# Earlier zeros for the PE fillers, two more fillers, and masks built by selections alone

## The chip, the cores and the metric

One core of a Trainium2 chip runs the whole program in one launch. The metric is the device time of that launch in microseconds (us). A kernel is run several times, and its time is the median of its runs. One further execution is recorded by the hardware profiler; every duration and start below is from that execution.

## The reference, cut to what matters

Four layers work on x (2048 tokens of 448 numbers, bfloat16). Layers 0 and 2 are attention over a local, dilated window, layers 1 and 3 are a bilinear GLU. Each adds its result to x.

```python
def A(x, wqkv, wo):                       # 16 heads of 28
    q, k, v = split(x @ wqkv)
    idx = pos[:, None] - 2 * arange(8)    # 8 keys: this token and every second one before it
    logits = einsum(q, k[idx]) * 28 ** -0.5, -1e9 where idx < 0
    return (softmax(logits) @ v[idx]) @ wo
def B(x, w_gate, w_up, w_down):           # F = 1792
    return ((x @ w_gate) * (x @ w_up)) @ w_down
x = x + A(layernorm(x)); x = x + B(layernorm(x))
x = x + A(layernorm(x)); x = x + B(layernorm(x))
```

## The kernel before

The kernel holds x in SBUF as 16 blocks of 128 tokens, even tokens in the first eight and odd tokens in the last eight, so that a dilation of two becomes a plain local window of eight. Each layer is cut into chunks of 256 or 512 tokens. `SEQ` gives the order in which chunks are planned, but what each engine runs, and in which order, is written out: `ORDER` has a list of operation numbers for each of the five queues (TensorE "pe", ScalarE "act", VectorE "dve", GpSimd "pool", SyncE "sp"), and `BANKS` gives the PSUM banks of each matmul group. An operation's number is its position in the sequence of `sc.add` calls. There is no planner left: an engine takes its list from front to back, and before each operation waits on semaphores for what that operation depends on. A dependence on an earlier operation of the same engine is also waited for by semaphore, except on TensorE. The `est` and `prio` arguments are read by nobody when an order is written out.

What comes before the first attention chunk matters here:

- SyncE issues the loads: x in five pieces, the rows of `wqkv` for V (`WV`), and those for Q and K into `stage`, which is the tile `hT` before the GLU uses it (line 444, four loads `("stg", c)`).
- VectorE takes five memsets, then the layer norm of the first blocks: `bn_stats` (line 582), `bn_aggr` (584), and the scaling into `xn_sb` (603). ScalarE makes `rstd` between them (585, 587).
- TensorE transposes the scaled blocks through an identity matrix (`ident`, lines 613 and 617). ScalarE or VectorE copies the result to `xnTa` (624, 627).
- VectorE and ScalarE spread the staged weights into the padded layout `WQK` (521), six copies and two. The first matmuls of Q and K wait for all eight and for the transposed blocks.
- TensorE has nothing to do at first. It runs `WARM + FILL` filler matmuls of 128 by 512 on `warm`, a slice of `hT` that VectorE sets to zero (line 513, operations 47 to 62): eleven ahead of the first transposes, three ahead of the second, two ahead of the third. Their results are never read.
- GpSimd sets constants and builds three masks `MK` (128 keys by 72 queries, kind 0 for the first group, 2 for the one over the middle, 1 for all others). The exponentials of the attention are cut by a minimum with the mask (line 853): very large where a key is in the window, zero elsewhere. The five parts of the masks are made in `MT`, also a slice of `hT`: one memset, then 16 selections of 128 by 72 (`affine_select`, line 491) in five chains, then three additions (495) that put the half for the first 64 keys and the half for the last 64 together. GpSimd's list runs the chains interleaved, with the other constants between them; the identity's memset and selection stand in the middle. The first writes of `hT` by the GLU wait for the masks (`war`), because `MT` lies there.

On TensorE almost every later operation is a pair of matmuls on the two row halves of the array, issued by the helper `pair` (line 351), so that line 351 covers Q and K, V, gate and up, down, and the output projection.

Of the kernel before, what the change touches and what calls it, by code (L numbers as in the profile page):

```python
# [57 lines left out]
WARM = 8  # L58
FILL = 8
# [36 lines left out]
def grp_nc(g):  # L96
# [8 lines left out]
        "47 48 49 50 51 52 53 54 55 56 57 112 58 59 60 109 61 62 127 210 130 211 240 133 136 241 204 228 205 229 200 234 201 154 235 230 198 231 202 199 151 "  # L105
        "203 232 157 160 233 215 193 354 178 355 249 352 220 353 350 175 184 351 181 254 244 496 245 498 196 497 499 575 500 576 501 571 266 572 267 271 356 "
        "369 357 370 502 276 503 379 373 569 374 570 573 574 401 384 308 302 305 314 288 311 289 320 326 338 317 323 396 526 335 397 406 520 329 521 332 515 "
        "341 516 344 345 548*3.5/346 347 531 588 418 589 419 448 445 457 451 463 543 460 544 553*1.2.4.5/442 472 469 475 454 599*1.3.5/466 481 593 565 478 566 "
        "484 485 594 486 487 665 604*1.2.4.5/662 677 689 674 490 621*2.4.5/491 668 492 742 736 493 737 743 738 626*3.5/740 616 739 617 686 741 701 671 680 759 "
        "692 760 698 683 695 638 755 639 704 756 705 765 706 707 779*1.3.5/826 710 838 823 711 829 712 713 770 784*1.2.4.5/835 841 853 850 847 859 896 900 820 "  # L110
        "901 897 980 898 894 899 895 977 989 796 918 986 797 1001 1013 919 992 998 1004 913 1010 914 832 924*5/844 856 1016 983 862 929 946 863 868 995 864 "
        "1007 865 869 951*2.4.5/941 870 871 942 1044 1035 1041 1053 1047 1056 963 1038 964 1019 1020 1059 1050 1062 1021 1022 1111 1105 1112 1109 1106 1124 "
        "1107 1110 1108 1065 1068 1071 1125 1074 1198 1135*2.4.5/1077 1078 1129 1201 1204 1079 1130 1157*2.4.5/1080 1213 1276 1278 1282 1277 1210 1279 "
        "1140*2.4.5/1283 1216 1207 1280 1228 1281 1162*1.2.4.5/1225 1152 1300 1153 1301 1222 1219 1311*1.3.5/1231 1234 1174 1295 1175 1296 1237 1333*2.4.5/1240 "
        "1241 1248 1316 1338 1249 1305 1250 1242 1306 1251 1243 1405 1402 1396 1408 1355*1.3.5/1420 1328 1350 1399 1329 1351 1432 1417 1414 1426 "
        "1360*1.2.4.5/1411 1423 1429 1435 1446 1438 1439 1447 1372 1440 1373 1448 1449 1477 1441 1474 1486 1498 1510 1480 1492 1483 1504 1542 1495 1554 1507 "
        "1545 1489 1557 1569 1581 1548 1501 1513 1551 1516 1517 1566 1560 1563 1524 1525 1575 1578 1526 1518 1572 1519 1527 1584 1587 1590"
    ),
    "act": (
        "14 106 107 102 103 118 119 113 110 124 128 125 131 63 70 137 242 243 212 142 143 213 236 209 155 207 239 190 148 191 149 237 166 206 167 158 161 238 "  # L120
        "172 217 173 216 179 360 251 250 359 176 358 255 225 226 259 260 246 247 263 264 505 578 273 272 296 297 361 371 372 277 507 380 381 285 375 286 402 "
        "281 309 282 303 386 306 403 315 389 393 312 390 394 321 327 339 318 324 527 528 426 336 427 407 408 330 522 333 342 432 433 411 412 517 415 416 549 "
        "550 532 540 536 537 590 541 449 446 452 464 458 461 554 443 558 646 473 470 559 647 476 652 562 455 720 721 563 653 600 601 482 467 479 726 727 663 "
        "666 605 678 690 675 613 609 610 614 622 669 623 744 627 628 631 632 745 635 746 687 636 672 702 804 810 811 805 681 693 761 699 684 696 767 766 781 "
        "780 827 839 878 884 885 879 824 830 971 771 972 772 836 786 842 775 776 789 790 854 851 848 860 793 794 905 821 981 1089 1090 902 978 990 987 1002 "
        "1014 920 993 1005 999 1029 915 1011 833 925 845 926 1030 857 1017 984 930 948 947 934 935 938 996 939 1008 952 956 960 1095 957 1045 961 1036 1096 "
        "1042 1048 1054 1057 1039 1051 1182 1063 1183 1060 1188 1189 1116 1260 1113 1115 1114 1066 1069 1072 1266 1267 1075 1126 1199 1261 1137 1136 1202 1205 "
        "1158 1159 1214 1284 1211 1141 1287 1285 1217 1145 1146 1208 1149 1150 1229 1286 1226 1302 1171 1223 1167 1168 1220 1172 1313 1232 1312 1235 1297 1380 "
        "1381 1238 1334 1335 1386 1387 1339 1321 1325 1326 1322 1340 1343 1406 1403 1347 1397 1348 1344 1409 1356 1357 1421 1400 1433 1418 1415 1427 1464 1465 "
        "1412 1361 1424 1430 1458 1459 1436 1369 1370 1365 1366 1536 1478 1537 1475 1487 1499 1511 1481 1493 1484 1505 1543 1555 1496 1508 1546 1558 1570 1490 "  # L130
        "1549 1582 1502 1514 1552 1567 1561 1564 1576 1579 1573 1589"
    ),
    "dve": (
        "16 17 45 46 15 104 105 114 116 100 115 117 101 111 122 108 120 126 121 123 129 140 68 64 132 135 65 66 67 69 134 141 138 139 188 186 189 187 150 153 "
        "170 146 144 147 145 162 164 168 156 165 163 159 169 152 171 208 192 214 73 77 74 72 75 71 78 76 177 194 248 219 174 180 218 183 221 222 223 253 252 "
        "185 195 182 224 256 257 258 227 262 197 504 261 265 270 580 506 269 268 294 292 295 293 275 274 300 298 378 278 279 284 280 400 382 577 383 579 287 "
        "385 525 310 283 387 307 304 388 392 405 316 290 313 391 291 328 395 322 319 340 325 424 422 404 423 425 398 399 337 434 428 409 429 331 436 430 410 "
        "431 334 414 343 440 547 438 529 530 413 417 551 349 533 534 539 535 718 421 644 538 598 542 719 348 552 716 420 447 453 450 645 642 465 459 462 545 "
        "546 555 650 643 717 556 557 444 561 648 651 649 471 474 477 654 456 656 564 620 560 658 483 660 468 480 602 567 603 800 568 802 595 489 724 488 725 "
        "803 722 723 732 730 606 607 667 734 664 801 679 728 612 608 676 691 624 611 625 670 494 615 495 747 629 630 634 618 633 619 806 688 807 808 809 874 "  # L140
        "876 818 812 682 816 814 764 637 694 673 700 877 703 685 641 697 757 640 778 769 768 709 708 969 782 875 882 970 880 881 828 883 840 890 783 825 892 "
        "886 888 967 968 831 714 973 715 773 785 774 1085 787 788 837 843 1087 975 777 792 855 852 849 861 1086 795 903 822 1088 791 982 904 979 991 1099 988 "
        "799 1027 1003 1015 798 1025 994 1026 1028 1006 923 1000 1012 834 945 927 846 928 858 1033 1018 985 931 932 933 950 1097 937 940 997 936 1031 949 866 "
        "1009 1091 867 1093 953 954 959 955 1094 1092 872 943 1256 944 958 873 1037 1257 962 1043 1046 1180 1101 1258 1055 1058 1259 1040 1103 965 1178 1181 "
        "966 1184 1179 1185 1049 1186 1187 1052 1192 1064 1190 1023 1262 1061 1263 1196 1024 1264 1265 1194 1070 1134 1272 1067 1073 1076 1268 1270 1200 1139 "
        "1274 1156 1203 1138 1206 1131 1081 1083 1215 1212 1142 1160 1143 1144 1148 1161 1147 1209 1218 1151 1230 1163 1164 1165 1170 1310 1155 1227 1154 1166 "
        "1224 1376 1169 1221 1173 1332 1315 1377 1378 1314 1236 1379 1176 1233 1177 1382 1383 1239 1384 1385 1390 1388 1337 1336 1392 1318 1317 1319 1320 1394 "
        "1324 1327 1323 1307 1341 1354 1346 1254 1342 1252 1244 1246 1407 1404 1398 1349 1345 1410 1422 1358 1331 1359 1330 1401 1456 1457 1352 1434 1353 1454 "
        "1455 1462 1416 1460 1463 1461 1419 1472 1362 1363 1413 1364 1470 1425 1368 1431 1466 1428 1437 1371 1468 1367 1374 1532 1533 1375 1534 1535 1540 1442 "
        "1538 1444 1476 1488 1500 1452 1482 1450 1512 1485 1494 1506 1544 1479 1556 1497 1509 1547 1559 1571 1583 1491 1503 1515 1550 1568 1553 1565 1562 1580 "  # L150
        "1577 1574 1530 1520 1522 1528 1585 1588 1591"
    ),
    "pool": (
        "24 44 22 39 28 21 40 18 29 32 35 25 20 26 23 41 19 33 36 34 37 30 27 42 38 31 43"
    ),
# [224 lines left out]
def build(nc, A_x, A_wqkv, A_wo, B_w_gate, B_w_up, B_w_down, out):  # L380
# [55 lines left out]
    def one(fn, key=None):  # L436
        return [(fn, key)]
# [56 lines left out]
    def madd(dst, a, b, key, deps):  # L494
        sc.add("pool", one(lambda E: E.tensor_tensor(MK[:, dst, :], MT[:, a, :], MT[:, b, :], ALU.add), key), 300, deps=deps, prio=-39)

# [611 lines left out]
```

## Time and profile before

| what | value |
|---|---|
| runs before, us | 384.62, 385.69, 384.62 |
| median, us | 384.62 |
| the profiled execution's own time, us | 384.94 |
| its span, first to last instruction, us | 383.2 |
| PE (TensorE matmul) busy | 376.2 us, 98% of the span |
| DVE (VectorE) busy | 289.0 us, 75% |
| ACT (ScalarE) busy | 204.0 us, 53% |
| POOL (GpSimd) busy | 5.9 us, 31 instructions, all before 6.53 us |
| granted TensorE clock | 1.0 |

A row of the timeline gives the start, the time from there to the end of the last instruction of the group, the engine, the line and the operation, and in brackets how long the engine had been idle before and what ended that. Instructions of one engine overlap at their ends, so a group's time is not the sum of its members. The profiled execution took 1.74 us more than its span, and 0.32 us more than the median.

### The profile page before, as it was taken

How to read it: one execution, taken by the hardware profiler on the slowest of the kernel's cores; microseconds unless marked ns; L12 is line 12 of the kernel's file. 1: busy time of each engine (PE TensorE's matmuls, PEld its weight loads, DVE VectorE, ACT ScalarE, POOL GpSimd, SP SyncE). 2: the span in 40 equal slices, each digit the busy share in tenths (PEclk: the TensorE clock that was granted, in tenths of full speed). 3: DMA queues.
4: the chain of work that ended last, by engine and by line, in shares of the span. 5: the costliest groups of instructions: out<-in, count | busy, mean ns of one | idle time of the engine just before them, and what ended most of it. 6: DMA issues, size and time to landing. Idle time of an engine off the chain costs nothing.

```text
span 383.2 us, 14252 instructions
## 1 busy us (share of the span) xinstructions
PE 376.2 (98%) x6320; PEld 210.8 (55%) x6320; DVE 289.0 (75%) x649; ACT 204.0 (53%) x388; POOL 5.9 (2%) x31
## 2 busy tenths in 40 slices
PE   7999999999999999999999999999999999999997
PEld 3545588644555445544766765545554444446664
DVE  7989999998977776787677985637998698455323
ACT  4997897655526562555465425547743635133310
POOL 6000000000000000000000000000000000000000
DMA  7755544710512034031101136220124004241003
GB/s 228 196 145 152 66 122 113 91 23 2 82 34 45 3 58 62 17 67 26 32 14 27 26 43 100 51 34 3 27 34 74 3 2 60 40 112 33 2 3 98
DMA packets 54882, 22.50 MB, mean 59 GB/s; under 512 B 45013, under 2 KB 54821, under 8 KB 54821
## 3 DMA queue, kind: packets, MB, share of 16 engines
q1 hardware_dynamic: 54676, 21.53, 28.4%
q8 instruction: 50, 0.82, 0.9%
q14 instruction: 12, 0.09, 0.1%
q10 hardware_dynamic: 144, 0.06, 0.1%
HBM read 8.54 MB, written 2.71 MB: 29 GB/s over the span
## 4 chain that ended last, share of the span: by engine, by line
PE 93%; DVE 2%; DMA 2%; ACT 1%; SPq 1%; issue 0%; DVEq 0%
PE ps L351 84%; PE ps L354 3%; PE ps L871 2%; PE ps L837 2%; DMA hT<-in_A_wqkv_dram 2%; PE ps L977 1%; SPq L444 1%; ACT E_sb L846 1%; ACT xnTa L627 0%; DVE Qz L823 0%; DVE xn_sb L603 0%; DVE R_sb L896 0%; PE ps L617 0%; ACT qk L712 0%; DVE E_sb L853 0%
## 5 line engine op out<-in xcount | busy, mean ns | idle before, releaser
L351 PE MATMUL ps<-xnTb,WGU 64*128 64x512 bf16 (+1 forms) x1894 | 172.4, 332 | 0.0
L351 PEld LDWEIGHTS ps<-xnTb,WGU 64*128 64x128 bf16 x1894 | 92.3, 94 | 69.3 <-ACT g_sb L962 1.0
L962 ACT ACTIVATE g_sb<-ps 128x512 bf16<-128x512 f32 (+1 forms) x140 | 70.2, 509 | 84.4 <-PE ps L351 64.6
L965 DVE TENSOR_TENSOR hT<-g_sb,ps 128x512 bf16<-128x512 bf16 (+1 forms) x140 | 78.3, 575 | 47.1 <-ACT g_sb L962 44.5
L351 PE MATMUL ps<-WD,hT 64*128 64x448 bf16 x812 | 82.8, 349 | 0.0
L351 PEld LDWEIGHTS ps<-WD,hT 64*128 64x128 bf16 x812 | 38.9, 94 | 35.5 <-issue 0.7
L351 PE MATMUL ps<-xnTa,WQK 64*128 64x512 bf16 (+1 forms) x494 | 53.5, 352 | 0.4 <-ACT qk L712 0.2
L926 DVE TENSOR_TENSOR x_sb<-x_sb,ps 128x448 bf16<-128x448 bf16 x62 | 37.2, 613 | 13.7 <-PE ps L351 13.5
L846 ACT ACTIVATE E_sb<-ps,shift_sb 128x1024 bf16<-128x1024 f32 (+1 forms) x36 | 37.1, 1068 | 12.6 <-PE ps L837 12.5
L603 DVE TENSOR_SCALAR xn_sb<-x_sb,mv,rstd 128x512 bf16<-128x512 bf16 (+1 forms) x64 | 36.0, 578 | 5.9 <-ACT rstd L587 5.7
L582 DVE BATCH_NORM_STATS2 st<-x_sb 128x6 f32<-128x448 bf16 x64 | 38.6, 616 | 1.5 <-DMA x_sb<-in_A_x_dram 1.1
L351 PEld LDWEIGHTS ps<-xnTa,WQK 64*128 64x128 bf16 x494 | 23.0, 94 | 22.4 <-ACT xnTa L627 0.6
L712 ACT ACTIVATE qk<-ps 128x1024 bf16<-128x1024 f32 (+1 forms) x27 | 25.4, 958 | 16.4 <-PE ps L351 16.3
L351 PE MATMUL ps<-wo_g,oT 64*128 64x448 bf16 x250 | 28.6, 349 | 0.0
L853 DVE TENSOR_TENSOR E_sb<-E_sb,MK 128x1024 bf16<-128x1024 bf16 (+1 forms) x36 | 23.4, 659 | 5.3 <-ACT E_sb L846 5.2
L897 ACT ACTIVATE R_sb<-R_sb 128x480 f32<-128x480 f32 (+1 forms) x34 | 20.2, 600 | 11.0 <-DVE R_sb L896 10.9
L909 DVE TENSOR_TENSOR oT<-O_sb,R_sb 128x480 bf16<-128x480 f32 (+3 forms) x36 | 22.1, 626 | 4.3 <-ACT R_sb L898 4.2
L351 PE MATMUL ps<-WV,xnTa 64*128 64x336 bf16 (+3 forms) x252 | 24.0, 304 | 0.2
L896 DVE STREAM_SHUFFLE R_sb<-O_sb 128x480 f32<-128x480 f32 (+1 forms) x34 | 22.9, 693 | 0.0
L585 ACT ACTIVATE lnv<-mv,eps_sb 128x2 f32<-128x2 f32 (+1 forms) x33 | 9.3, 292 | 22.1 <-DVE mv L584 22.1
L898 ACT ACTIVATE R_sb<-R_sb 128x480 f32<-128x480 f32 (+1 forms) x34 | 20.0, 600 | 0.6
L882 ACT ACTIVATE O_sb<-ps 128x512 f32<-128x512 f32 (+3 forms) x19 | 10.4, 559 | 14.1 <-PE ps L871 14.1
(61 smaller groups left out, 218.2 us busy)
## 6 DMA issues: line engine op xcount, KB each, us to landing
out_dram<-x_sb SPq DMA_DIRECT2D x15, 112.0 KB, 1.9
x_sb<-in_A_x_dram SPq DMA_DIRECT2D x3, 448.0 KB, 7.2
hT<-in_A_wqkv_dram SPq DMA_DIRECT2D x4, 224.0 KB, 5.5
WGU<-in_B_w_gate_dram SPq DMA_DIRECT2D x4, 224.0 KB, 3.5
WGU<-in_B_w_up_dram SPq DMA_DIRECT2D x4, 224.0 KB, 4.1
WD<-in_B_w_down_dram SPq DMA_DIRECT2D x2, 448.0 KB, 3.7
WGU<-in_B_w_gate_dram SPq DMA_DIRECT2D x2, 336.0 KB, 4.5
WGU<-in_B_w_up_dram SPq DMA_DIRECT2D x2, 336.0 KB, 4.6
```

The costliest lines, as they stand in the source:

```text
L351: return lambda E: E.matmul(out(), lhs(), rhs(), start=start, stop=stop)
L582: sc.add("dve", one(lambda E, B=B: E.bn_stats(st6[:, B, :], x_sb[:, B, :]), ("bn", li, B)), 525.0, deps=[("x", li - 1, B)] + ([("xn", li - ...
L603: sc.add("dve", one(lambda E, B=B, dst=dst, src=src: E.tensor_scalar(dst, src, mv[:, B, 0:1], rstd[:, B:B + 1], ALU.subtract, ALU.mult), ( ...
L712: return E.activation(dst, src, ACT.Copy) if hasattr(E, "activation") else E.tensor_copy(dst, src)
L846: return E.activation(E_sb[:, slot, 2 * hp:2 * hp + 2, 0:w], ps[:, b0:b0 + 2, 0:w], ACT.Exp, bias=shift_sb[:, 0:1], scale=SCALE)
L853: return E.tensor_tensor(e, e, MK[:, kind, 0:nc].unsqueeze(1).unsqueeze(1).to_broadcast([128, 2, w // nc, nc]), ALU.min)
L896: sc.add("dve", one(lambda E: E.stream_shuffle(R_sb[:, rs, 0:w], O_sb[:, os_, 0:w], [DH] * 32), ("Rs", li, qb)), dve_est(w) + 20.0, deps=[ ...
L897: sc.add("act", one(lambda E: E.activation(R_sb[:, rs, 0:w], R_sb[:, rs, 0:w], ACT.Ln), ("Rl", li, qb)), act_est(w, False), deps=[("Rs", l ...
L909: return E.tensor_tensor(oT[:, :, a % HALF:a % HALF + z - a], O[:, :, a - tok:z - tok], R_sb[:, rs, 0:w].rearrange("p (h n) -> p h n", h=4 ...
L926: sc.add("dve", one(lambda E: E.tensor_tensor(x_sb[:, B, :], x_sb[:, B, :], ps[:, bk[w], 0:D], ALU.add), ("x", li, B)), dve_est(D), deps=[ ...
L962: sc.add("act", one(lambda E, gs=gs, bk=bk: E.activation(g_sb[:, gs, 0:nt], ps[:, bk[0], 0:nt], ACT.Copy), ("G", li, j, fc)), act_est(nt), ...
L965: sc.add("dve", one(lambda E, gs=gs, bk=bk, fc=fc: E.tensor_tensor(hT[:, fc, hs, 0:nt], g_sb[:, gs, 0:nt], ps[:, bk[1], 0:nt], ALU.mult), ...
```

## The change

`WARM` and `FILL` go from 8 to 9, so there are 18 fillers. The two new ones stand ahead of the first transposes (13 instead of 11). VectorE's list begins with the memset of `warm`, which came after the other memsets before. GpSimd's list is now in the order of the calls: the identity first, then the constants, then the masks. The masks no longer use `MT`: one memset fills all of `MK`, and 13 selections on 64 partitions each cut it in place, the lower half by two (three for kind 2) and the upper half by two. All 13 hang in one chain, each waiting for the one before. There are no additions. The GLU's first writes of `hT` no longer wait for the masks. The program has four operations fewer, so the later numbers in `ORDER` and `BANKS` are lower by four; apart from what is named here, the sequence on every engine and the banks are as they were.

```diff
-WARM = 8
-FILL = 8
+WARM = 9
+FILL = 9
 ORDER: "pe"
-"47 48 49 50 51 52 53 54 55 56 57 112 58 59 60 109 61 62 127 ...
+"41 42 43 44 45 46 47 48 49 50 51 52 53 108 54 55 56 105 57 58 123 ...
 ORDER: "dve"
-"16 17 45 46 15 104 105 ...
+"15 16 17 39 40 100 101 ...
 ORDER: "pool"
-"24 44 22 39 28 21 40 18 29 32 35 25 20 26 23 41 19 33 36 34 37 30 27 42 38 31 43"
+"18 19 38 20 21 22 23 24 25 26 27 28 29 30 31 32 33 34 35 36 37"
...
-    MT = hT[:, 10, 0, 0:5 * 72].rearrange("p (k n) -> p k n", k=5)
...
-    memset("pool", MT, BIG, "i_mt", 300)
-
-    def sel(t, conds, key):
-        dep = "i_mt"
+    memset("pool", MK[:], BIG, "i_mk", 300)
+
+    later = [(W - 1 - 64, 1, -1), (64, -1, 1)]
+    dep = "i_mk"
+    for lo, dst, conds in ((0, 0, [(W - 1, 1, -1), (0, -1, 1)]), (0, 1, [(-1, 1, -1), (W, -1, 1)]), (0, 2, [(-1, 1, -1), (W, -1, 1), (55, 0, -1)]),
+                           (64, 0, [(W - 1 - 56, 1, -1), (56, -1, 1)]), (64, 1, later), (64, 2, later)):
         for n, (base, cm, step) in enumerate(conds):
-            k = key if n == len(conds) - 1 else (key, n)
-            sc.add("pool", one(lambda E, base=base, cm=cm, step=step: E.affine_select(MT[:, t, :], MT[:, t, :], [[step, 72]], ALU.is_ge, 0.0, base=base, channel_multiplier=cm), k), 300, deps=[dep], prio=-40)
+            k = f"c_mk{dst}" if lo and n == len(conds) - 1 else ("mk", dst, lo, n)
+            sc.add("pool", one(lambda E, dst=dst, lo=lo, base=base, cm=cm, step=step: E.affine_select(MK[lo:lo + 64, dst, :], MK[lo:lo + 64, dst, :], [[step, 72]], ALU.is_ge, 0.0, base=base + cm * lo, channel_multiplier=cm), k),
+                   245, deps=[dep], prio=-40)
             dep = k
-
-    def madd(dst, a, b, key, deps):
-        sc.add("pool", one(lambda E: E.tensor_tensor(MK[:, dst, :], MT[:, a, :], MT[:, b, :], ALU.add), key), 300, deps=deps, prio=-39)
...
-    madd(0, 0, 1, "c_mk0", ["i_x0", "i_y0"])
...
-                war = hslot_users.get((hs, "prev"), WQKR + [f"c_mk{k}" for k in range(3)])
+                war = hslot_users.get((hs, "prev"), WQKR)
```

## The prediction

> **What bounds the kernel now.** I read the page's busy times first, then the chain that ended last, then that chain in the head, then the timeline of the first 22 us.
>
> ```profile
> PE 376.2 (98%) x6320; PEld 210.8 (55%) x6320; DVE 289.0 (75%) x649; ACT 204.0 (53%) x388; POOL 5.9 (2%) x31
> ...
> PE 93%; DVE 2%; DMA 2%; ACT 1%; SPq 1%; issue 0%; DVEq 0%
> ```
>
> TensorE (PE) is the bound, and 93% of the last chain lies on it. The change touches none of that work; it only touches what runs before 7 us. So the question is when TensorE's dense work begins. The chain, in order of time, says so (start, duration, what):
>
> ```profile
> 4.73 0.45 SPq L444
> 5.17 0.04 issue
> 5.22 5.76 DMA hT<-in_A_wqkv_dram
> 10.97 0.02 issue
> 11.00 0.58 ACT WQK L521
> 11.57 0.49 ACT xnTa L627
> 12.07 0.05 issue
> 12.11 3.86 PE ps L351 x48
> ```
>
> Up to 12.11 us the chain is SyncE's issues, then the last load of staged Q and K weights (landed at 10.97), then two ScalarE operations, then the first Q and K matmuls. No filler, no memset, no mask is on it. A second limit sits beside the first. ScalarE follows VectorE's layer norm back to back from 9.04 us, and that waits for x at 7.07:
>
> ```profile
> 1.08 0.81 DVE L474 MEMSET wo_g<- 128x896 uint32 x1 [0.16 <-issue]
> 2.43 0.27 DVE L474 MEMSET hT<- 128x256 uint32 x1
> 2.76 4.66 PE L513 MATMUL ps<-hT 128*128 128x512 bf16 x11 [2.76 <-DVE hT L474]
> 2.89 0.63 DVE L582 BATCH_NORM_STATS2 st<-x_sb 128x6 f32<-128x448 bf16 x1 [0.19 <-DMA x_sb<-in_A_x_dram]
> 4.31 1.39 POOL L491 TENSOR_SCALAR_AFFINE_SELECT hT<-hT 128x72 bf16<-128x72 bf16 x7
> 5.66 0.87 POOL L495 TENSOR_TENSOR MK<-hT 128x72 bf16<-128x72 bf16 x3
> 5.74 0.94 DVE L603 TENSOR_SCALAR xn_sb<-x_sb,mv,rstd 128x512 bf16<-128x512 bf16 x1
> 7.00 0.46 PEld L613 LDWEIGHTS ps<-ident,xn_sb 128*128 128x128 bf16 x4 [0.28 <-DVE xn_sb L603]
> 7.07 0.63 DVE L582 BATCH_NORM_STATS2 st<-x_sb 128x6 f32<-128x448 bf16 x1 [0.38 <-DMA x_sb<-in_A_x_dram]
> 7.47 0.81 PE L513 MATMUL ps<-hT 128*128 128x512 bf16 x3
> 9.22 0.62 DVE L582 BATCH_NORM_STATS2 st<-x_sb 128x6 f32<-128x448 bf16 x1
> ```
>
> The reader is to see three things. The eleven fillers run at a pitch of about 0.425 us (4.25 us from 2.75 to 7.00, where the next weights are loaded); the three after them at (0.81 - 0.379) / 2 = 0.215 us, 0.379 being the shortest filler. TensorE thus reaches double rate at about 7.0, some 4.25 us after its first matmul, though the granted clock column reads 1.00 throughout. VectorE's first scaling takes 0.94 us beside GpSimd's additions, while the twelve of its kind before 24 us have a median of 0.41. And VectorE then idles 0.38 us until x lands at 7.07.
>
> **The change part by part.**
>
> VectorE's memsets: the same five, in another order, 0.86 to 2.70 in total. The one of `hT` now ends at 0.86 + 0.27 = 1.13, and by the old delay of 0.06 us TensorE starts at 1.19 instead of 2.76, 1.57 us earlier. The constants that move back by 0.27 us are wanted late: `eps_sb` at 3.77, the `qmask` at 21.37. The first `bn_stats` still waits for x at 2.89, 0.19 us after the memsets. Cost: nothing; without the cover of 0.19, at most 0.27 us, and that again hidden by the 0.38 before 7.07.
>
> Two more fillers: 2 x 0.425 = 0.85 us at the slow pitch, 0.43 at the fast one. Thirteen at the slow pitch run from 1.19 to 1.19 + 13 x 0.425 = 6.72, earlier than the old 7.0. The first transposes come then, 0.3 us sooner, and ScalarE's first copy to `xnTa` (7.67) too. Nothing behind that moves: the next VectorE and ScalarE steps wait for x at 7.07. Gain on the path: 0. If TensorE is fast sooner, the fillers end sooner and it only waits.
>
> TensorE's ramp: fast from 1.19 + 4.25 = 5.44 if it counts from the first matmul, still at 7.0 if it is tied to fixed instants. Both lie 5 us ahead of 12.11, so the dense work meets the same rate either way. The Trainium skill ("TensorE: Matmul & The Clock Gate", section "What's actually happening") says that the gate looks at free-running windows of about 3.4 us, and one busy window opens it, so the wait varies between executions. By it the wait would lie between 3.4 and 6.8 us (estimate from that page); the trace, 4.25, agrees. The sum by that rule is the same in an execution like the profiled one; its other consequence is the second case below.
>
> GpSimd: one memset, 16 selections and three additions give way to one memset and 13 selections. Between selections before, the pitch was 0.19 us (1.39 less one of 0.245, over six gaps), but a selection never waited for the one just before. Now each does. From below 13 x 0.19 = 2.5 us. From above, the wait of VectorE's `qmask` memset on its predecessor (1.84 with 0.06 long, next start 1.97) adds 0.07: 13 x 0.315 = 4.1 us. I take the upper end, since the dependence is of that kind. The constants ahead of them, by their pitches, need 0.15 + 0.25 + 0.15 + 0.47 + 0.21 + 0.22 + 0.05 + 0.23 = 1.73 us (the 0.23 lies between memsets of 128 and 360 columns). GpSimd ends between 0.79 + 1.73 + 2.5 = 5.0 and 6.6 us; before, at 6.53. The masks are first read at 24.1 us, so 17 us cover any of this. The identity is ready near 1.4 instead of 4.35, and is wanted after the fillers. `v_sb` constants come a little later than 2.1 and are wanted at 12.05. The wait that leaves the GLU's first writes was met at 6.5, long before: 0.
>
> VectorE's slow scaling: 0.94 - 0.41 = 0.53 us come back if GpSimd is done by 5.7, nothing if its chain runs to 6.6. Either way what is late next is x at 7.07, so on the path 0.
>
> **Sum.** 384.94 for the profiled execution, plus 0, against its median 0.32 lower: 384.62, forecast 384.6. What I can't see is bounded so: towards gain, if the 0.53 passed straight through, and TensorE's idle stretch ahead of 12.11 (0.57) with it, 384.62 - 0.53 - 0.57 = 383.5. Towards loss, two scalings stalled like the one before, 2 x 0.53 = 1.06, 385.7.
>
> **The rivals.** 0.3% of the time, 1.15 us, is about what a measurement of this kernel can tell from no change.
>
> *Late ramp relieved.* One run of before took 385.69, 1.07 more. If in such runs the ramp ends after the fillers of the first batch, five later fillers cost 5 x 0.21 = 1.05 us more, TensorE gets late for the transposes, and some of it reaches 12.11. Starting 1.57 us earlier would remove that. The new kernel then takes 384.6 or a little less, and the old one in a fresh comparison up to 385.7: 0.28%, at the edge of telling. For it speaks the spread; against it, that two of three runs and the profile show none. 0.18, of it 0.10 faster.
>
> *The head gets shorter.* If the landing at 10.97 only happens to coincide and VectorE and ScalarE set the start, the freed 0.53 us and the idle 0.57 give 383.5. Against it: VectorE idles for x at 7.07 and again at 13.12. 0.10, of it 0.08 faster.
>
> *TensorE falls back (slower).* Fillers end earlier, between about 5.9 (5.44 and two at the fast pitch) and 6.7, and TensorE then waits for the scaling, which ends at 6.15 to 6.7. If this thinner stretch up to 9.3 makes the rate drop again, the Q and K stage from 12.11 repeats a ramp: 4.25 us of work at half rate, 2.1 us lost, 386.7. It decides once the gap suffices to lose the rate. The trace has a pause of 0.57 us ahead of 12.11 without a drop (pairs of 512 columns go on at 0.215 us), and the expected gaps are 0.8 at most. 0.09. The same page ("Why this matters for your kernels") puts the gap that closes the gate at about 3 us, which speaks against this rival; its "Part 4: PE-mode transpose" says transposes do not count as busy, which speaks for it. No gap of that length is in the stretch.
>
> *GpSimd's chain lasts longer.* If selections on 64 partitions, each waiting, cost over 0.35 us, GpSimd works past 7.07 and stalls VectorE's busy stretch: 385.7. 0.06, half of it slower.
>
> *The change doesn't do what it says,* TensorE still starting near 2.7 because of another wait: its first matmul waits for VectorE alone, so 0.02, and 384.6.
>
> **How the numbers follow.** Forecast, head hidden: 0.55 at 384.6. Within 0.3%: 0.55 + 0.08 + 0.02 + 0.03 + 0.02 = 0.70. Faster: 0.10 + 0.08 = 0.18. Slower: 0.09 + 0.03 = 0.12. The range 383.5 to 385.7 takes in both bounds of the unknown costs and leaves out the fallen rate and the larger gains.
>
> **What would show it.** In the new profile: the first filler at about 1.2; the first transposes at 6.2 to 6.8; VectorE's `bn_stats` still waiting for x near 7.07; the chain through the weight load landing near 11; the first Q and K matmul near 12.1, and pairs at 0.215 us from there; GpSimd done by 6.6. I am wrong if that first matmul starts before 11.5 or after 12.6, or if the chain in the head runs through VectorE or the fillers.

## The result and the profile after

The changed kernel took 384.27 us in the median of 19 runs (383.88 to 384.89), the kernel before 385.21 us in 19 runs beside it (384.53 to 386.76). The ratio is 0.9977, interval 0.9967 to 0.9986: 0.23% faster, inside the 0.3% that the prediction called no change, but clear of zero. (Here and below the ratio and its interval come from the single runs, so a ratio need not equal the quotient of the two medians.) The spread shrank too, from 2.2 to 1.0 us. The profiled execution took 383.93 us with a span of 382.2, 1.0 less than before.

From the page of the changed kernel, the busy times and the last chain by engine:

```profile
PE 376.7 (99%) x6322; PEld 211.2 (55%) x6322; DVE 288.2 (75%) x649; ACT 203.8 (53%) x388; POOL 5.2 (1%) x25
...
PE 93%; DVE 3%; ACT 1%; DMA 1%; issue 1%; SPq 0%; DVEq 0%
```

TensorE is the bound as before, with 0.5 us more work (the two fillers). Its chain in the head, in order of time:

```profile
2.22 4.08 DMA x_sb<-in_A_x_dram
6.30 0.02 issue
6.33 0.04 DVE st L571
...
10.20 0.74 DVE WQK L510 x4
10.94 0.33 DVE xnTa L616
...
11.42 3.86 PE ps L351 x48
```

The dense work starts at 11.42 instead of 12.11. The chain leads back through VectorE to the landing of x's blocks 4 to 7 at 6.30. (x comes in six loads, not five. Three bring blocks 0 to 3, and this one, issued fourth, is called x's second load below.) In the profile of before, VectorE's wait for it ended at 7.07. From the wait's end to the first Q and K matmul it is 12.11 - 7.07 = 5.04 us before and 11.42 - 6.33 = 5.09 after. So the 0.69 us in this pair of profiles came with a load that landed earlier, and the change doesn't touch how that load is issued. The timeline of the changed kernel:

```profile
0.92 0.27 DVE L473 MEMSET hT<- 128x256 uint32 x1 [0.92 <-PEq L1082]
1.25 5.55 PE L502 MATMUL ps<-hT 128*128 128x512 bf16 x13 [1.25 <-DVE eps_sb L473]
2.62 4.09 POOL L492 TENSOR_SCALAR_AFFINE_SELECT MK<-MK 64x72 bf16<-64x72 bf16 x13
5.92 0.38 DVE L592 TENSOR_SCALAR xn_sb<-x_sb,mv,rstd 128x512 bf16<-128x512 bf16 x1
6.33 0.63 DVE L571 BATCH_NORM_STATS2 st<-x_sb 128x6 f32<-128x448 bf16 x1
6.64 0.39 PE L602 MATMUL ps<-ident,xn_sb 128*128 128x128 bf16 x4
```

TensorE starts at 1.25, 1.51 us earlier; the fillers fill the time to the first transposes; GpSimd's chain of selections has a pitch of (4.09 - 0.245) / 12 = 0.32 us and ends at 6.71; and the first scaling takes 0.38 us beside those selections.

One pair of profiles can't say whether the median moved for this reason or for another. That is what the experiments are for.

### The profile page after: what moved, and what is told of

Same layout as the page of the kernel before. It is cut to its first block, busy times and chain, and to the rows that moved or that the text cites. A ratio compares the mean times of both kernels' runs of the same rounds, so it can differ in the third digit from the quotient of the medians.

```text
span 382.2 us, 14253 instructions
## 1 busy us (share of the span) xinstructions
PE 376.7 (99%) x6322; PEld 211.2 (55%) x6322; DVE 288.2 (75%) x649; ACT 203.8 (53%) x388; POOL 5.2 (1%) x25
## 4 chain that ended last, share of the span: by engine, by line
PE 93%; DVE 3%; ACT 1%; DMA 1%; issue 1%; SPq 0%; DVEq 0%
PE ps L351 85%; PE ps L354 3%; PE ps L860 2%; PE ps L826 2%; PE ps L966 1%; DMA x_sb<-in_A_x_dram 1%; DVE xn_sb L592 1%; ACT E_sb L835 1%; DVE Qz L812 0%; DVE R_sb L885 0%; SPq L443 0%; DVE st L571 0%; ACT xnTa L616 0%; PE ps L606 0%; ACT qk L701 0%
## 5 line engine op out<-in xcount | busy, mean ns | idle before, releaser
L592 DVE TENSOR_SCALAR xn_sb<-x_sb,mv,rstd 128x512 bf16<-128x512 bf16 (+1 forms) x64 | 35.4, 567 | 6.4 <-ACT rstd L576 6.2
```

Of the source, the lines that this page charges most:

```text
L592: sc.add("dve", one(lambda E, B=B, dst=dst, src=src: E.tensor_scalar(dst, src, mv[:, B, 0:1], rstd[:, B:B + 1], ALU.subtract, ALU.mult), ( ...
```

## The experiments

Each kernel was run 12 times (9 for `e7_one`) beside 29 to 35 runs of the kernel before on the same chip, the second profile of before once.

### Which half does it: masks, or zeros and fillers

`e1_masks` has the new masks, with the zeros and the fillers as before:

```diff
-WARM = 9
-FILL = 9
+WARM = 8
+FILL = 8
 dve: -"15 16 17 39 40 ..."   +"16 17 39 40 15 ..."
 pe:  -13 fillers ahead of the first transposes   +11
```

> The masks of the change alone: GpSimd's new list, but the zeros of the fillers are VectorE's fifth memset again and there are 16 fillers. Medians so far 385.21 before, 384.27 changed. Theory S (stall: GpSimd's additions held VectorE's first scaling for 0.53 us): the scaling takes 0.4 us and the time is 384.3 to 384.6, the whole gain or most of it. Theory R (ramp: TensorE's earlier start is what counts): 385.2, no gain. Theory L (landing: x's second load, blocks 4 to 7, landed at 6.30 instead of 7.07 in one profile, by chance): the time follows the landing, 384.6 to 385.2 in the median, and the profile's first matmul of Q and K comes 5.05 us after that landing.

Measured: 385.37 us against 384.89 before, ratio 1.0004 (0.9990 to 1.0017). No gain. Its chain:

```profile
2.43 0.28 DVE hT L473
...
2.76 4.87 PE ps L502 x11
7.63 0.43 PE ps L602 x4
8.06 0.91 PE ps L502 x3
...
11.85 0.76 PE ps L351 x8
...
12.66 3.86 PE ps L351 x48
```

Here the chain runs from the late memset of `hT` through the fillers, all at the slow pitch, and then through TensorE's queue without a pause. TensorE reached double rate only behind 8 us (the four transposes still take 0.43; in the chain of `e2_fillers` below they take 0.22), and the dense work starts 12.66 - 6.98 = 5.68 us after VectorE's wait for x, 0.6 more than in the two profiles above. The fillers were the last thing waited for.

`e2_fillers` is the complement, with the old masks:

```diff
-WARM = 8
-FILL = 8
+WARM = 9
+FILL = 9
 dve: -"16 17 45 46 15 ..."   +"15 16 17 45 46 ..."
 pe:  -11 fillers ahead of the first transposes   +13
```

> The zeros first and two more fillers alone, with the old masks, additions included. Theory S: 385.2, no gain, and VectorE's first scaling still takes about 0.94 us. Theory R: 384.3, the whole gain, and less spread between runs. Theory L: 384.6 to 385.2, by the landing.

Measured: 383.95 us against 384.89, ratio 0.9979 (0.9966 to 0.9992). The whole gain, without the new masks. The chain is again that of the fillers, but earlier:

```profile
1.25 5.70 PE ps L513 x13
6.95 0.22 PE ps L613 x4
...
11.53 3.86 PE ps L351 x48
```

The stall was there in full, since the additions were still beside the first scaling (`5.66 1.03 DVE L603` in its timeline), and the gain came all the same; the chain doesn't run through it. The theory of the stall falls twice.

`e3_adds` asks the same from the other side: the changed kernel with three GpSimd additions put back.

```diff
+    scr = hT[:, 10, 0, 0:5 * 72].rearrange("p (k n) -> p k n", k=5)
+    for n in range(3):   # behind the tenth selection, each waiting for the one before
+        ... E.tensor_tensor(scr[:, n, :], ones32[:, 0:72], ones32[:, 0:72], ALU.add) ...
```

> The changed kernel with three GpSimd additions of 128 by 72 put back after its tenth selection, on data nobody reads, so that they run from about 5.8 to 6.9 us beside VectorE's first scaling; each waits for the one before. Theory S: the scaling takes 0.8 to 1.0 us again, everything behind it on VectorE is 0.4 to 0.5 us later, and the time is 384.7 to 385.1. Theory R and theory L: 384.3, as the changed kernel.

Measured: 384.13 us against 384.89, ratio 0.9982 (0.9970 to 0.9995): the gain stays. But the means failed, as the scaling took 0.38 us; additions with waits between them did not hold it. As a test of the stall's price this run says nothing; `e2_fillers` does.

### How far the head varies by itself

`c_before` is the kernel before once more, for its profile.

> The kernel before, unchanged, for a second profile. Theory L: x's second load lands at another time than 7.07, anywhere from 6.2 to 7.3. Theories S and R: it lands near 7.07 again, or VectorE's wait ends when the stalled scaling ends, near 6.7.

It took 386.14 us. Its chain, and rows of its timeline:

```profile
5.29 7.44 DMA hT<-in_A_wqkv_dram
...
13.87 3.86 PE ps L351 x48
```

```profile
2.76 4.87 PE L513 MATMUL ps<-hT 128*128 128x512 bf16 x11 [2.76 <-DVE hT L474]
5.70 0.43 DVE L603 TENSOR_SCALAR xn_sb<-x_sb,mv,rstd 128x512 bf16<-128x512 bf16 x1
7.94 0.63 DVE L582 BATCH_NORM_STATS2 st<-x_sb 128x6 f32<-128x448 bf16 x1 [1.81 <-DMA x_sb<-in_A_x_dram]
```

The same kernel, and x's second load is 0.87 us later than in its first profile, the last weight load 1.75 us (12.72 against 10.97). The landing at 7.94 is outside the 6.2 to 7.3 expected. The additions did not stall the scaling this time (0.43). The eleven fillers took 4.87 us, as in `e1_masks`, against 4.66 in the first profile: the late ramp occurs in the kernel before too, but in this execution the weights came later still.

### The zeros, the fillers, and what each is worth

Four kernels on one chip: the zeros first alone, the two fillers alone, four fillers fewer, and the changed kernel with a single filler.

```diff
 e4_zeros  dve: -"16 17 45 46 15 ..."   +"15 16 17 45 46 ..."        (before; 11 fillers ahead)
 e5_two    pe:  -11 fillers ahead of the first transposes   +13      (before; zeros late)
 e6_seven  pe:  -11 fillers ahead of the first transposes   +7       (before; zeros late)
 e7_one    pe:  -13, 3 and 2 fillers   +1, 0 and 0                   (changed; zeros first)
```

> One half of the TensorE side: the zeros first, but the old 16 fillers, 11 ahead of the first transposes, and the old masks. Theory P (place: the fillers ahead of the first transposes stand in the way of the transposes when x lands early, so their end counts): they end at 1.25 + 11 x 0.427 = 5.95 or sooner, ahead of the scaled block, and the time is 383.9 to 384.2, all of the gain. Theory Q (ramp: an earlier and unbroken start brings the double rate sooner, and the added fillers keep it going until the first block is there): TensorE pauses 0.3 to 0.8 us before the transposes, the ramp ends later in some runs, 384.2 to 384.8, with a wider spread than with both halves.

> The other half: two more fillers, the zeros still VectorE's fifth memset, old masks. Theory P: the fillers end 0.43 to 0.85 us later, at 7.9 to 8.3, and the time is 385.3 to 385.8 against 384.9 before. Theory Q: the ramp starts when it did, and what follows finds TensorE at double rate or closer to it: 384.7 to 385.0, no loss.

> The kernel before with four fillers fewer: 7 ahead of the first transposes, zeros in their old place. Theory P: the fillers end at 2.76 + 7 x 0.427 = 5.75, out of the way, and the time is 383.9 to 384.3, the gain of the change by another road. Theory Q: the ramp doesn't end sooner, 4.25 to 5.5 us after 2.76 or later still because TensorE pauses: 384.9 to 385.6.

> The changed kernel with one filler in all. Theory P alone, fillers being only in the way: 383.9 to 384.3. Theory Q: the ramp falls into the transposes, V matmuls and the Q and K stage; if those from about 8.5 us on start it, it ends 2.75 to 5.5 us later, at 11.2 to 14, and half of what it takes behind 11.4 is lost: 385 to 386.5.

| kernel | median, us | before, us | ratio (95%) |
|---|---|---|---|
| e4_zeros | 384.79 | 385.30 | 0.9990 (0.9980 to 1.0000) |
| e5_two | 385.30 | 385.30 | 0.9993 (0.9982 to 1.0005) |
| e6_seven | 385.78 | 385.30 | 1.0014 (0.9996 to 1.0032) |
| e7_one | 386.08 | 385.30 | 1.0026 (1.0014 to 1.0039) |

The theory that fillers are only in the way (P) fails: it wanted `e6_seven` and `e7_one` at 384.3 or less. Theory Q has `e4_zeros` and `e7_one` right, but `e5_two` and `e6_seven` came out above its 384.7 to 385.0 and 384.9 to 385.6. One filler is clearly worse, and its chain shows the price, TensorE at half rate from the transposes to the V matmuls:

```profile
7.98 0.62 PE ps L602 x4
...
10.33 1.89 PE ps L351 x9
12.22 0.43 PE ps L606 x12
12.65 4.75 PE ps L351 x40
```

In the timeline the first Q and K matmul comes at 13.55, 6.56 us after the load. Not all of the loss is there: the time less the span is 2.09 us in the median of this kernel's runs and 1.72 in those of before beside it, so 0.37 of the 0.78 us lies outside the span, and nothing on record says why. Two fillers more without early zeros gain nothing that shows: in its profile the chain is the fillers', and the dense work starts 5.46 us after the load:

```profile
2.76 5.25 PE ps L513 x13
...
12.57 3.86 PE ps L351 x48
```

The zeros alone bring perhaps half of the gain; the interval reaches from nearly all to none.

### The load, tested directly

Four kernels on another chip: the changed one again, the changed one with VectorE's second scaling ahead of the step that waits for x, the changed one with 16 fillers, and the changed one with x's second load issued later.

```diff
 e8_reorder  dve: -"... 107 118 104 116 122 ..."   +"... 107 104 118 116 122 ..."
 e9_sixteen  pe:  -13 fillers ahead of the first transposes   +11
 e10_xlate   sp:  -"1 2 0 7 8 9 ..."   +"1 2 0 8 9 7 ..."
```

> The changed kernel again, beside the three that follow. Theory H (two paths: the first Q and K matmul comes about 5.0 us after the landing of x's second load, or about 5 us after the fillers ahead of the first transposes end, whichever is later; the change shortens the second path): 0.2% to 0.3% faster than before, and in the profile the first Q and K matmul 4.9 to 5.1 us behind the landing. Theory T (TensorE alone: the start and the end of the ramp set it, the landing does not): the same gain, with no fixed distance to the landing.

> The changed kernel with one step of VectorE moved: the second scaling goes ahead of the bn_stats that waits for x's second load. By theory H VectorE then works while it waits: with the landing near 7.0 the first Q and K matmul is 0.3 us earlier, with a landing at 6.3 it is 0.3 later; median 0 to 0.3 us less than the changed kernel, less spread. Theory T: the second transposes come up to 0.4 us sooner, 0 to 0.4 us less.

> The changed kernel without its two fillers: zeros first, new masks, 11 ahead of the first transposes. Theory H: the fillers end at 5.95 at the latest, the landing decides alone, and the time equals the changed kernel's within 0.2 us. Theory T: the pause before the transposes delays the ramp in some executions, 0.3 to 0.6 us more than the changed kernel.

> The changed kernel with x's second load issued behind the two V weight loads instead of ahead of them, 1.02 us later on SyncE's queue. Theory H: it lands 0.6 to 1.2 us later and the first Q and K matmul follows it at 5.0 us; the time grows by 0.5 to 1.1 us, to about that of before or above. Theory T: TensorE's fillers and ramp are as they were, the time grows by at most 0.2 us.

| kernel | median, us | before, us | ratio (95%) |
|---|---|---|---|
| c_after | 384.15 | 384.76 | 0.9992 (0.9979 to 1.0004) |
| e8_reorder | 384.15 | 384.76 | 0.9988 (0.9970 to 1.0005) |
| e9_sixteen | 384.89 | 384.76 | 1.0006 (0.9989 to 1.0023) |
| e10_xlate | 385.67 | 384.76 | 1.0030 (1.0007 to 1.0052) |

`e10_xlate` settles the load: 1.5 us more than the changed kernel beside it, with the same fillers. Its chain:

```profile
3.21 4.96 DMA x_sb<-in_A_x_dram
8.17 0.02 issue
8.20 0.04 DVE st L571
...
12.33 4.59 PE ps L351 x56
```

VectorE's wait ends at 8.20, and by the timeline Q and K start at 13.06, 4.86 us later. The 1.5 us are more than the 0.5 to 1.1 that theory H expected. Four of its twelve executions (386.87 to 388.23) show a mean granted clock of 0.995 or 0.996, the other eight (384.89 to 386.01) 1.0; the median of those eight, 385.59, is still 1.44 us above the changed kernel. In the repeat of the changed kernel, 385.48 us in that execution, the weights landed last:

```profile
5.68 5.68 DMA hT<-in_A_wqkv_dram
11.37 0.02 issue
...
12.51 3.86 PE ps L351 x48
```

So the changed kernel too has late executions. The repeat's interval includes 1, where 0.2% to 0.3% faster was expected. With 16 fillers the median (384.89, range 383.67 to 386.81) is 0.74 us above that with 18 (384.15, 383.87 to 385.53); the ranges overlap. Theory H allowed 0.2 us, so the path account alone may not cover it; the 0.3 to 0.6 of theory T is nearer. `e8_reorder` doesn't beat the changed kernel.

### All profiles together

| profile | VectorE's wait for x ends | first Q and K matmul | distance | span less that start | chain in the head |
|---|---|---|---|---|---|
| before | 7.07 | 12.11 | 5.04 | 371.1 | weights landing |
| c_before | 7.94 | 13.87 | 5.93 | 370.5 | weights landing |
| e1_masks | 6.98 | 12.66 | 5.68 | 371.1 | zeros, fillers |
| e5_two | 7.11 | 12.57 | 5.46 | 370.9 | zeros, fillers |
| e6_seven | 7.11 | 11.97 | 4.86 | 370.4 | x landing |
| e4_zeros | 7.72 | 12.68 | 4.96 | 371.3 | x landing |
| e2_fillers | 6.61 | 11.53 | 4.92 | 370.3 | zeros, fillers |
| after | 6.33 | 11.42 | 5.09 | 370.8 | x landing |
| c_after | 7.35 | 12.51 | 5.16 | 371.3 | weights landing |
| e3_adds | 6.74 | 11.68 | 4.94 | 370.8 | x landing |
| e8_reorder | no such wait | 11.67 | | 370.7 | weights landing, VectorE |
| e9_sixteen | 6.95 | 11.93 | 4.98 | 371.1 | x (block 1), VectorE, ScalarE |
| e10_xlate | 8.20 | 13.06 | 4.86 | 370.8 | x landing |
| e7_one | 6.99 | 13.55 | 6.56 | 370.7 | x, then TensorE at half rate |

(In `e2_fillers` the stalled scaling ended last, so 6.61 is no landing.) From the first Q and K matmul to the end it is 370.3 to 371.3 us in all of them. What differs is the start. But for `e7_one`, these profiles fit the latest of three: x's second load plus about 5 us, TensorE's own queue behind the zeros and the fillers, and the last weight load plus about 1.1 us. The change shortens the second alone. It doesn't say what the two added fillers are for: with the same early zeros, 11 end sooner than 13. Compare the executions with the longest fillers: dense work at 12.66 and 12.57 with the zeros late, at 11.53 with zeros first and 18 fillers.

## Why the prediction was right, and where it was not

- *Its own signs.* The time lay in the range, but two signs of being wrong appeared in the new profile: the first Q and K matmul at 11.42, ahead of 11.5, and a chain through VectorE.
- *What bounds the kernel.* Right: the end is the start of the dense work plus a fixed stretch.
- *"No filler, no memset, no mask is on it."* True of both profiled executions of before, wrong as a forecast for all of them. In `e1_masks` and `e5_two`, with the zeros late as before, the chain of the head is memset, fillers, transposes. This is the step that failed: the forecast's gain of 0 on the path, taken from one execution. The gain was 0.94 us in the first comparison, 0.61 in the medians of the second, whose interval includes none.
- *Late ramp relieved.* This rival, not the forecast, is nearest to what the runs bear out, at about its price: 384.6 "or a little less" was 384.27, and the old kernel was at 385.2 rather than its 385.7. The median of 384.62 that I started from was drawn from three runs, and 19 moved it by 0.6; that is luck, and more than the mechanism it is why the forecast point lay so close.
- *Zeros at 1.19.* 1.25: VectorE's memset started at 0.92 instead of 0.86. The row puts the release down to the memset behind (`eps_sb`), which ended at 1.20. *13 fillers to 6.72:* 6.80. *First transposes 0.3 us sooner:* 0.61 (6.64 against 7.25). The prediction set the end of thirteen against the start of the last of eleven; end against end it is 7.42 against 6.72. By the same slip three fillers, not two, were left at 5.44, to end near 6.1. *GpSimd 0.315 us a step, done by 6.6:* 0.32 and 6.71.
- *VectorE's 0.53 us.* Hidden, as said: it stayed in `e2_fillers` (1.03 us), and the gain came all the same. It doesn't belong to every execution with the additions: 0.43 in the second profile of before.
- *TensorE falls back.* It did not in the changed kernel: all 31 of its runs show a clock of 1.0. In the profile of `e10_xlate` TensorE paused 1.99 us, and the four transposes behind it took 0.40 us as usual (its row is `9.19 0.40 PE L602 MATMUL ps<-ident,xn_sb 128*128 128x128 bf16 x4 [1.99 <-DVE xn_sb L592]`). The Trainium skill ("TensorE: Matmul & The Clock Gate", section "Why this matters for your kernels") puts the harmful gap near 3 us. No profile here has fillers and then a pause that long. But a clock of 0.995 or 0.996 stands beside four runs of `e10_xlate`, one of `e9_sixteen` (386.81) and one of `e6_seven` (387.53), each 1.2 us or more above the median of its kernel. If the clock was at half there, 0.004 to 0.005 of 386 us is a stretch of 3.1 to 3.9 us that loses half as much, 1.6 to 2.0 (estimate), against the rival's 2.1. No trace of those runs is kept, so where it lay is not shown.
- *The landing near 7.07 as a fixed limit.* It is the largest variable of the head: 6.3 to 7.9 us in profiles whose loads are issued alike. That was not in the prediction, and it makes up the difference between the two profiles first compared. Whether the masks have a part in it is open: with the old ones the wait ended at 7.07 to 7.94 in five profiles and at 6.61 in a sixth, with the new ones at 6.33 to 7.35 in six.

Shown is that the zeros and fillers together bring the gain (`e2_fillers`) and the masks alone do not (`e1_masks`). Open is how the gain is shared between them, and by what mechanism the two fillers add to it: zeros first with 16 fillers gave 0.9990 (`e4_zeros`) and 1.0006 (`e9_sixteen`), both intervals reaching 1. And `e1_masks` bounds the masks' own part only to between 0.1% faster and 0.17% slower.

## What to carry to other kernels

A chain in a profile is the chain of one execution. Where several paths end within a microsecond of each other, as here the loads and the fillers, each is last in some executions, and shortening one moves the median and the spread although the chain in hand does not show it. Fillers for TensorE pay when they start as early as their operand can be there and end when the real work is ready: late ones stand in its way, too few leave it at half rate.

## What the runs showed of the hardware

The time from TensorE's first matmul to double rate is not fixed. With the pitch of 0.427 us before and 0.215 after, and 0.379 for the last one, 13 fillers in 4.32 us (`e3_adds`) mean a change after (4.32 - 0.379 - 12 x 0.215) / 0.212 = 6.4 fillers, 2.7 us; in 4.65 us (`e10_xlate`) after 3.4 us. In the first profile of before it was 4.25 us. Nine of the packed traces hold a record of the granted clock. (The clock column shows 1.00 ahead of the first entry too.) The record has full clock from 4.01 us in `e3_adds`, 4.66 in `e10_xlate`, 6.79 in `e2_fillers` and 8.47 in `e1_masks`: 2.76, 3.41, 5.54 and 5.71 us after the first filler. Full clock then lasts 372.05, 375.47 or 378.88 us, in steps of 3.41 us.

The Trainium skill ("TensorE: Matmul & The Clock Gate", section "What's actually happening") explains such a scatter by free-running windows of about 3.4 us, one of which must be busy. The steps agree with it, but the 2.76 us is shorter than one window. Counted back by 3.41 us from the change, the window of `e3_adds` began at 0.60; TensorE was busy from 1.25, 81% of it, and that was enough. In `e1_masks` the window from 1.64 to 5.05, busy from 2.76 or 67%, was not.

GpSimd's additions held VectorE's scaling in five of the six profiles that have them back to back (0.85 to 1.03 us) and not in the sixth (0.43, `c_before`), although there too they started within 0.03 us of the scaling. Beside selections the same scaling took 0.38 to 0.42.
